# Sparse attention, a 2-D DFT and a two-layer network on one core: values of two query tiles in one task, DFT matmuls of full width, and another order

## The chip, the cores and the metric

The program runs on one core of one Trainium2 chip. The metric is device time in microseconds (us). A time beside a kernel's name is the median of its runs; the profile is of one further execution, whose own time is given with it.

## The reference

Eight batches. Attention first: eight heads of width 64, 32 global and 512 local rows. A global query sees all 544 keys; a local query sees the 32 global keys and the local keys at most 32 rows away.

```python
s_g = scale * np.matmul(q_g, k_all.transpose(0, 1, 3, 2))
out_g = np.matmul(sm(s_g), v_all)
mask = np.abs(pos[:, None] - pos[None, :]) <= window        # window = 32
s_l = np.concatenate([s_lg, np.where(mask, s_ll, -1e9)], axis=-1)
out_l = np.matmul(sm(s_l), np.concatenate([v_g, v_l], axis=2))
```

The 544 x 512 result of a batch then goes through a 2-D Fourier transform of which the real part is kept, a normalisation, and two layers of 2048 and 512 columns:

```python
mixed = np.real(np.fft.fft(np.fft.fft(x, axis=1), axis=2))
u = x + mixed
un = (u - mu) / np.sqrt(var + 1e-06)
out = u + np.maximum(un @ w_ch1, 0.0) @ w_ch2
```

## The kernel before

Every large product is made of three float16 products (high times high, high times low, low times high), so that its accuracy is near float32. The weights come in as 64-bit numbers and are split on the chip.

**Attention.** The unit is a pair of heads (32 pairs, four to a batch). Its 512 local queries are four tiles of 128; two tiles are a half (64 halves). `scores` (L646, L656) multiplies a half's queries with its keys in matmuls that take 64 rows and 64 stationary columns. `masked` (VectorE) and `exps` (ScalarE) follow; for each single tile `p_hi` (ScalarE) and `p_lo` (GpSimd) split the exponentials into `ph`, and `turn` (L688) transposes them by DMA into `pl`. `values` (L691 to L707) multiplies one transposed tile by the values: 20 matmuls with 64 stationary columns each. Two neighbouring `values` write one PSUM bank, `bk`, and `norm` (VectorE) divides a half's result. The next half may write `bk` only after that `norm`. `g_scores` (L734 to L741) and `g_values` (L776) do the same for the global queries of two pairs, with 64 and with 32 stationary columns.

**DFT.** `d_first` (L973, L975) runs five times a batch: four times eight matmuls with 128 stationary columns, and once eight with one column, for the frequency that stands alone. `d_second` (L1003, L1005) runs six times a batch, for three row tiles `kt` and two parts `cs`: row tiles 0 and 1 have 128 stationary columns, row tile 2 has 18. With `cs` 0 it adds one matmul on a constant of 64 rows (`alt`, L1005). `d_as`, `d_df`, `d_addp` and `d_addv` add the result to the input, which makes the rows of the network.

**Network.** These rows come in 17 chunks of 256. VectorE and ScalarE normalise a chunk and split it (`l_hi` is L1075, `l_lo` is L1079), and a DMA transposes it (`l_turn`, L1102). TensorE then runs 16 `f_first` tasks (L1128, 12 matmuls with 256 moving columns) and 16 `f_second` tasks (L1146, 6 matmuls with 512) for each chunk, 272 of each in all, with 128 stationary columns in every matmul.

**What sets the order.** `run` lists all tasks with their engine, an assumed duration, what they need and what they free. `Plan.order` goes through an assumed time line and gives each engine a fixed order; a due time decides between tasks that could start, and the table `BIAS` shifts the due times. Each engine then runs its instructions in exactly that order, and waits where an input is late. The assumed durations thus decide on the order alone.

Of the kernel before, what the change touches and what calls it, by code (L numbers as in the profile page):

```python
# [20 lines left out]
P = 128  # L21
# [33 lines left out]
def shape_constants():  # L55
    r = np.arange(P)[:, None]
    k = np.concatenate([np.arange(1, 144, 2), [0], np.arange(271, 144, -2), np.arange(2, 143, 2), [272, 0], np.arange(270, 143, -2)])[None, :]
    used = np.arange(NK)[None, :] != 72
    tt = np.concatenate([np.arange(129, 144), np.arange(415, 400, -1), [0, 272]])[:, None]
    c1 = np.zeros((P, 2, 2, NK), np.float16)  # L60
    c1t = np.zeros((96, 2, NK), np.float16)
    c2 = np.zeros((P, 2, 2, 2, NH), np.float16)
    for i, fn in enumerate((np.cos, np.sin)):
        for j, a in enumerate(_hi_lo(fn(2 * np.pi * ((r + 1) * k % T) / T) * used)):
            c1[:, i, j] = a
        hi, lo = _hi_lo(fn(2 * np.pi * (tt * k % T) / T) * used)
# [24 lines left out]

def cold(key):

    n, i = key[0], key[1] if len(key) > 1 else 0
    if n == "scores":
        return 2.4 if i < 8 * NRAW else 0.8
    if n == "g_scores":
        return 3.7 if i < 2 * NRAW else 1.2
    if n == "values":
        return 0.8  # L100
    if n == "g_values":
        return 1.1
    return COLD.get(n)
# [16 lines left out]
HALVES = "scores masked exps norm".split()  # L120
QUARTERS = "p_hi p_lo turn p_turn p_copy values".split()
GROUPS = "s_total scales0 scales g_scores g_max g_exp g_hi g_lo g_turn g_copy g_values g_norm".split()


def place(key):

    n, i = key[0], key[1] if len(key) > 1 else 0
    if n in ("load_consts", "l_load"):
        return ("K", 0), 0
    if n in WHOLE:  # L130
# [22 lines left out]
class Plan:  # L153
# [12 lines left out]
    def dues(self):  # L166
        nxt = {k: [] for k in self.tasks}
        for t in self.tasks.values():
            for a in t.data:
                nxt[a].append(t)  # L170
        done = set()
        for root in self.tasks:
            stack = [(root, iter(nxt[root]))]
            if root in done:
                continue
            while stack:
                k, it = stack[-1]
                for n in it:
                    if n.key not in done:
                        stack.append((n.key, iter(nxt[n.key])))  # L180
                        break
                else:
                    stack.pop()
                    if k not in done:
                        done.add(k)
                        t = self.tasks[k]
                        lat = t.dur + (4.0 if t.eng == "SP" else 0.3)
                        t.due = min([t.due] + [n.due - lat for n in nxt[k]])
        for t in self.tasks.values():
            t.due -= t.early + BIAS.get((t.key[0], t.stage), 0) + BIAS.get(t.unit, 0)  # L190

    def order(self):
        self.dues()
        left = {k: len(set(t.after)) for k, t in self.tasks.items()}
        nxt = {k: [] for k in self.tasks}
        for t in self.tasks.values():
            for a in set(t.after):
                nxt[a].append(t)
        engines = ("PE", "DVE", "ACT", "POOL", "SP")
        free = dict.fromkeys(engines, 0.0)  # L200
        ready = {e: [t for t in self.tasks.values() if t.eng == e and not left[t.key]] for e in engines}
        insts, out, dma, bank, t0 = {}, [], 0.0, ("", 0.0), None
        now, count = 0.0, 0
# [47 lines left out]
        while count < len(self.tasks):  # L251
            best = None
            for e in engines:
                low = max(now, free[e])
                if best is not None and low > best[0][0]:
                    continue
                for t in ready[e]:
                    at = max(low, t.base)
                    if best is not None and (at, t.cls, t.due) >= best[0]:
                        continue  # L260
                    at = max(at, ok_at(t))
                    if at < LATE and (best is None or (at, t.cls, t.due) < best[0]):
# [36 lines left out]
class Kern:  # L299
# [64 lines left out]
    def load_consts(self):  # L364
        nc, c = self.nc, self.cp
        for n, shape in (("c1", [P, 2, 2, NK]), ("c1t", [96, 2, NK]), ("c2", [P, 2, 2, 2, NH]), ("alt", [64, NH])):
# [1081 lines left out]
```

## Time and profile before

| | before |
|---|---|
| median of 3 runs | 1026.47 us (1025.48 to 1026.83) |
| profiled execution, its own time | 1026.17 us |
| its span, first to last instruction | 1024.3 us |
| TensorE matmuls busy | 930.3 us (91%) in 12115 matmuls |
| VectorE, ScalarE, GpSimd busy | 528.6, 546.5, 577.9 us |
| granted TensorE clock, mean | 0.953 |

The span is the stretch between the first and the last instruction that were recorded; 1.87 us of the execution's time lie outside it. Matmuls are pipelined, and their recorded durations overlap. What a task takes of TensorE is therefore read here from start to start: the first matmul of the next task minus the first matmul of this one.

### The profile page before, as it was taken

Reading aid. Unit: us, or ns where it says so; the run is one execution under the profiler, and the core shown is the slowest. Engines: PE = TensorE matmul, PEld = TensorE weight load, DVE = VectorE, ACT = ScalarE, POOL = GpSimd, SP = SyncE. Lnnn points to the kernel's source line nnn. Section 1 sums busy time; section 2 is a strip of 40 time slices with the busy share of each in tenths; the row PEclk is TensorE's granted clock in tenths of the full one; section 3 lists DMA queues with packets and bytes.
Section 4 is the critical chain, followed back from the end, with each engine's and each line's share of the span. In section 5 each row is a group of like instructions: output and inputs, shape, how many; then the busy total and the mean of one; then the engine's idle time right before and its main releaser. Section 6 shows DMA issues by size and latency. Waiting matters only on the chain.

```text
span 1024.3 us, 29886 instructions
## 1 busy us (share of the span) xinstructions
PE 930.3 (91%) x12115; PEld 640.3 (63%) x12115; DVE 528.6 (52%) x1609; ACT 546.5 (53%) x1234; POOL 577.9 (56%) x976
## 2 busy tenths in 40 slices
PE   2663459999999999999999999999999999999996
PEld 1442337666666766666676667667667766667673
DVE  5987786147644664446557444783534433221111
ACT  6997768867776656864676667453421311111010
POOL 5599775888868577958757795882416111010000
PEclk9985558999999999999999999999999999999999
DMA  9998998347886566783876797244161201201000
GB/s 334 304 251 235 273 182 187 109 120 134 162 179 151 132 140 151 171 167 105 149 165 130 129 204 162 78 93 103 34 138 48 62 13 53 62 1 42 1 22 21
DMA packets 215794, 133.12 MB, mean 130 GB/s; under 512 B 167808, under 2 KB 185312, under 8 KB 215656
## 3 DMA queue, kind: packets, MB, share of 16 engines
q1 hardware_dynamic: 215656, 131.21, 55.5%
q8 instruction: 95, 1.56, 0.6%
q14 instruction: 43, 0.35, 0.1%
HBM read 64.97 MB, written 18.35 MB: 81 GB/s over the span
## 4 chain that ended last, share of the span: by engine, by line
PE 80%; DMA 6%; DVE 4%; POOL 3%; ACT 2%; SPq 2%; issue 1%; POOLq 0%; ACTq 0%; DVEq 0%
PE ps L1128 34%; PE acc L1146 34%; PE bk L704 3%; DMA vf<-in_v 2%; PE S L656 2%; PE bk L707 1%; PE S L646 1%; DMA raw<-in_moe_w_ch 1%; PE psd L1003 1%; DMA vS<-vN 1%; DMA pl<-ph 1%; PE S L739 1%; PE S L1003 1%; PE psd L973 1%; PE pvg L776 1%
## 5 line engine op out<-in xcount | busy, mean ns | idle before, releaser
L1128 PE MATMUL ps<-uh,wh 128*128 128x256 f16 x3264 | 383.2, 273 | 0.0
L1146 PE MATMUL acc<-wh,h 128*128 128x512 f16 x1632 | 375.1, 379 | 1.5 <-DVE h L1137 1.5
L1128 PEld LDWEIGHTS <-wh 128*128 128x128 f16 x3264 | 313.4, 98 | 52.5 <-issue 1.1
L1146 PEld LDWEIGHTS <-h 128*128 128x128 f16 x1632 | 154.6, 98 | 167.9 <-DVE h L1137 2.0
L1133 ACT ACTIVATE h<-ps 128x512 f16<-128x512 f32 x136 | 81.0, 596 | 289.0 <-PE ps L1128 281.8
L1137 DVE SCALAR_TENSOR_TENSOR h<-ps,h 128x512 f16<-128x512 f32 x136 | 93.7, 689 | 254.5 <-ACT h L1133 254.3
L682 POOL TENSOR_TENSOR ph<-pe,ph 128x256 f16<-128x256 f32 x128 | 86.9, 679 | 46.7 <-ACT ph L678 29.4
L675 ACT ACTIVATE pe<-pe,nm 128x160 f32<-128x160 f32 x256 | 88.0, 416 | 20.2 <-DVE nm L666 20.1
L666 DVE CUSTOM_DVE_ANT_0 pe<-S,msk,z 128x160 f32<-128x160 f32 x192 | 62.2, 379 | 45.3 <-PE S L656 33.6
L704 PEld LDWEIGHTS <-pl 128*64 128x64 f16 x1536 | 47.8, 120 | 39.0 <-issue 23.5
L704 PE MATMUL bk<-vS,pl 128*64 128x65 f16 x768 | 56.7, 208 | 11.7 <-DMA vS<-vN 11.7
L704 PE MATMUL bk<-vN,pl 128*64 128x65 f16 x768 | 56.9, 207 | 8.7 <-DVE x L718 8.1
L596 POOL TENSOR_TENSOR vN<-vf,vN 128x640 f16<-128x640 f32 x32 | 43.7, 1367 | 28.8 <-ACT vN L592 28.7
L678 ACT ACTIVATE ph<-pe 128x320 f16<-128x320 f32 x128 | 55.2, 458 | 8.7 <-DMA pl<-ph 8.6
L1027 POOL TENSOR_TENSOR u<-u,asm 128x257 f32<-128x257 f32 x16 | 13.1, 816 | 75.4 <-DMA u<-xs 44.0
L707 PE MATMUL bk<-vN,pl 128*64 128x65 f16 x1024 | 52.6, 205 | 0.5 <-issue 0.5
L646 PE MATMUL S<-gr,qk 64*64 64x32 f32 x256 | 13.5, 287 | 34.4 <-DVE nm L666 27.4
L683 POOL TENSOR_TENSOR ph<-pe,ph 128x64 f16<-128x64 f32 x128 | 43.6, 341 | 0.0
L707 PEld LDWEIGHTS <-pl 128*64 128x64 f16 x1024 | 42.1, 121 | 0.6 <-issue 0.6
L481 POOL TENSOR_TENSOR wh<-wm,wh 128x512 f16<-128x512 f32 x32 | 36.9, 1159 | 5.5 <-ACT wm L474 3.9
L1151 DVE SCALAR_TENSOR_TENSOR u<-acc,ve,u 128x512 f32<-128x512 f32 x34 | 25.5, 751 | 27.2 <-PE acc L1146 27.0
L620 POOL TENSOR_TENSOR qT<-qk,qT 128x512 f16<-128x512 f32 x24 | 27.9, 1165 | 19.0 <-ACT qT L615 18.9
(212 smaller groups left out, 1492.6 us busy)
## 6 DMA issues: line engine op xcount, KB each, us to landing
qk<-in_qk SPq DMA_DIRECT2D x32, 512.0 KB
vf<-in_v SPq DMA_DIRECT2D x32, 320.0 KB
raw<-in_moe_w_ch SPq DMA_DIRECT2D x17, 512.0 KB
vS<-vN SPq DMA_DIRECT2D x64, 130.0 KB
xs<-x SPq DMA_DIRECT2D x32, 256.0 KB
out<-u SPq DMA_DIRECT2D x16, 512.0 KB
x<-xs SPq DMA_DIRECT2D x24, 256.0 KB
u<-xs SPq DMA_DIRECT2D x24, 256.0 KB
```

The source lines that it names most:

```text
L596: self.nc.gpsimd.tensor_sub(vN[:, :, 1, :, 0:64], self.st[p]["vf"], vN[:, :, 0, :, 0:64])
L666: nc.vector.tensor_tensor_reduce(self.per[(4 * p + j) % 4][:, h], S[:, h, 160 * n:160 * n + 160], self.msk[:, j], z[:, 8:9], 3e38, op0=ALU ...
L675: nc.scalar.activation(pe[:, h], pe[:, h], AF.Exp, bias=nm[:, n, h:h + 1], scale=-1.0)
L678: self.nc.scalar.activation(self.phr[i % NPH][:, :, 96:256], self.per[i % 4], AF.Copy)
L682: self.nc.gpsimd.tensor_sub(ph[:, :, 256:384], pe[:, :, 32:160], ph[:, :, 128:256])
L683: self.nc.gpsimd.tensor_sub(ph[:, :, 64:96], pe[:, :, 0:32], ph[:, :, 96:128])
L704: nc.tensor.matmul(pv[r, j % 2, h], pl[:, 3 * h + 1 + a, r], v, start=x == 0, stop=False)
L707: nc.tensor.matmul(pv[r, j % 2, h], pl[:, 3 * h, r], vN[:, 4, c, h], start=False, stop=c == 1)
L1128: nc.tensor.matmul(ps[:, q], wt[:, w, c0:c0 + P], uh[:, :, 4 * a + kt, :], start=n == 0, stop=n == 11)
L1133: self.nc.scalar.activation(h[:, 0], self.fps[c, fp], AF.Relu)
L1137: self.nc.vector.scalar_tensor_tensor(h[:, 1], self.fps.pop((c, fp)), 0.0, h[:, 0], op0=ALU.max, op1=ALU.subtract)
L1146: nc.tensor.matmul(self.acc_f[c, j], h[:, a, q, j * P:(j + 1) * P], self.w[1, f][:, w, :], start=f == 0 and a == 0 and w == 0, stop=f == 1 ...
```

## The change

Two neighbouring `values` become one task of 40 matmuls, which needs both transposed tiles. The transposed tiles get six buffers instead of four.

```diff
-        self.st[p]["pl", j] = pl = self.p3.tile([P, 6, P], F16, name="pl", bufs=4)
+        self.st[p]["pl", j] = pl = self.p3.tile([P, 6, P], F16, name="pl", bufs=6)
     def values(self, i):
-        nc, (p, j) = self.nc, divmod(i, 4)
+        nc, (p, half) = self.nc, divmod(i, 2)
...
+        for n in range(2):
+            j = 2 * half + n
+            pl = s.pop(("pl", j))
...
-                    nc.tensor.matmul(pv[r, j % 2, h], pl[:, 3 * h, r], vN[:, 4, c, h], start=False, stop=c == 1)
+                        nc.tensor.matmul(pv[r, n, h], pl[:, 3 * h, r], vN[:, 4, c, h], start=False, stop=c == 1)
```

In the DFT the lone frequency and row tile 2 are computed with 128 stationary columns, of which the same one and 18 result rows are used as before; the constants `alt` and `zr` get 96 rows, the added ones zero.

```diff
-    alt = np.zeros((64, NH), np.float16)
+    alt = np.zeros((96, NH), np.float16)
-        self.zr = c.tile([64, NK], F16, name="zr")
+        self.zr = c.tile([96, NK], F16, name="zr")
-                nc.tensor.matmul(po, eh[:, a, e:e + m], self.c1[:, cs, c, c0:c0 + n], start=k == 0, stop=False)
+                nc.tensor.matmul(po, eh[:, a, e:e + P], self.c1[:, cs, c, c0:c0 + n], start=k == 0, stop=False)
-                nc.tensor.matmul(po, z[:, a, o, k0:k0 + r], self.c2[:, cs, o, c, :], start=n == 0, stop=n == 2 and cs + o > 0)
+                nc.tensor.matmul(po, z[:, a, o, k0:k0 + P], self.c2[:, cs, o, c, :], start=n == 0, stop=n == 2 and cs + o > 0)
-                nc.tensor.matmul(po, self.zr[:, k0:k0 + r], self.alt, start=False, stop=True)
+                nc.tensor.matmul(po, self.zr[:, k0:k0 + P], self.alt, start=False, stop=True)
```

The order counts a change between the groups `scores`, `values`, `g_scores`, `g_values` and everything else as extra TensorE time, some assumed durations differ, the biases of chunk tasks share one entry, and the weights' transfers get units of their own. The table of biases is a new one throughout.

```diff
+FORM = {"scores": 1, "values": 2, "g_scores": 3, "g_values": 4}
+TURN = 0.105
+            if e == "PE" and FORM.get(t.key[0], 0) != form:
+                form = FORM.get(t.key[0], 0)
+                t.dur += TURN if t0 is not None else 2 * TURN
-BIAS = {('load_consts', 0): -57, ('K', 0): -100, ('w_load', 0): 112, ...
+BIAS = {('load_consts', 0): 246, ('K', 0): -151, ('w_load', 0): 102, ...
```

Line numbers of the kernel after are higher by 9 in the attention's preparation, by 8 at `g_values`, and by 11 at `d_second` and the network.

TensorE, row tile 2 of the DFT of batch 2 with `cs` 0 (`z0` is its stationary operand, `zr` the constant's, `wh` the network's weights), before:

```order
L1003 LDWEIGHTS z0_6009
L1003 MATMUL S_6414<-c2r_172,z0_6009 18x129
...
L1005 LDWEIGHTS zr_176
L1005 MATMUL S_6414<-altr_174,zr_176 18x129
...
L1128 LDWEIGHTS wh_1050
L1128 MATMUL ps1_6426<-uh_4468,wh_1050 128x256
```

After:

```order
L1014 LDWEIGHTS z0_6162
L1014 MATMUL psd_6561<-c2r_164,z0_6162 128x129
...
L1016 LDWEIGHTS zr_168
L1016 MATMUL psd_6561<-altr_166,zr_168 128x129
...
L473 MATMUL bk_131<-vac1_78,part_64 128x6
L1139 LDWEIGHTS wh_1155
L1139 MATMUL ps1_6450<-uh_4339,wh_1155 128x256
```

The first number of a matmul's shape is its stationary columns. The 18 have become 128, in the DFT's matmuls and in that on the constant.

TensorE, two `values` of one half at the start of chunk 2 (`pl` are the transposed tiles), before:

```order
L704 LDWEIGHTS pl_4225
L704 MATMUL bk_131<-vN_70,pl_4225 64x65
...
L1128 LDWEIGHTS wh_741
L1128 MATMUL ps1_4387<-uh_4059,wh_741 128x256
...
L704 LDWEIGHTS pl_4236
L704 MATMUL bk_131<-vN_70,pl_4236 64x65
```

After, a half that stands between two tasks of the network:

```order
L712 LDWEIGHTS pl_4871
L712 MATMUL bk_131<-vN_70,pl_4871 64x65
...
L712 LDWEIGHTS pl_4973
L712 MATMUL bk_131<-vS_71,pl_4973 64x65
...
L1139 LDWEIGHTS wh_1155
L1139 MATMUL ps1_5300<-uh_4037,wh_1155 128x256
```

Before, one `f_first` stood between the two tiles; after, the second tile's matmuls follow the first's without anything between.

ScalarE, the last instructions up to the second half of chunk 0 (L1075; `kT`, `kg`, `qk` and `qT` are the keys and queries of batch 2), before:

```order
L605 ACTIVATE qk2_97<-qk2_97,z_1971 128x512
L397 ACTIVATE ps1_2226<-raw_2138 128x512
L1075 ACTIVATE unh_2230<-un_2219 128x512
L402 ACTIVATE raw_2138<-raw_2138 128x512
L615 ACTIVATE qT_2235<-qk2_97 128x512
L626 ACTIVATE kg1_69<-gT_946,z_1971 128x64
L605 ACTIVATE qk0_95<-qk0_95,z_1971 128x512
L1075 ACTIVATE unh_2322<-un_2300 128x512
```

After (L1086 is that instruction now):

```order
L1021 ACTIVATE asm_2141<-psd_2076,dsc_1451 18x258
L1086 ACTIVATE unh_2144<-un_2138 128x512
L687 ACTIVATE ph_84<-pe1_86 128x2x160
L547 ACTIVATE junk_76,vac0_77<-vf1_73 128x640
L547 ACTIVATE junk_76,vac0_77<-qk0_95 128x512
L406 ACTIVATE ps1_2170<-raw_2013 128x512
L1086 ACTIVATE unh_2180<-un_2167 128x512
```

The preparation of batch 2's queries and keys stands behind chunk 0's second half now, no longer ahead of it.

## Rows read from the trace of the kernel before

**Rows 1.** Windows: busy time by engine, clock, DMA share and GB/s.

```profile
0.00:50.00 50.00, 22.73 (x430) 16.56 (x430) 36.02 (x118) 39.23 (x88) 27.83 (x56) 1.00 1.05 318
100.00:150.00 50.00, 24.12 (x404) 18.14 (x397) 41.44 (x100) 37.38 (x83) 38.40 (x57) 0.50 1.03 241
157.00:1015.00 858.00, 854.53 (x10690) 583.10 (x10688) 405.84 (x1233) 425.00 (x961) 460.63 (x797) 1.00 0.49 107
1015.00:1024.30 9.30, 0.00 (x0) 0.00 (x0) 0.37 (x1) 0.00 (x0) 0.00 (x0) 0.74 0.18 56
```

**Rows 2.** Waits of TensorE from 157 to 1015: total, times, longest.

```profile
PE acc L1146 <- DVE h L1137: 1.5, 1, 1.5
```

**Rows 3.** Timeline, network at the end: start, us, what, count.

```profile
1003.99 5.40 PE L1128 MATMUL ps<-uh,wh 128*128 128x256 f16 x48
1009.23 5.34 PE L1146 MATMUL acc<-wh,h 128*128 128x512 f16 x24
```

**Rows 4.** Timeline, TensorE at the start of chunk 2.

```profile
257.74 1.48 PE L1128 MATMUL ps<-uh,wh 128*128 128x256 f16 x12
259.15 0.22 PE L704 MATMUL bk<-vN,pl 128*64 128x65 f16 x1
...
259.59 0.61 PE L1128 MATMUL ps<-uh,wh 128*128 128x256 f16 x4
```

**Rows 5.** Timeline, TensorE, batch 2's DFT and a `g_scores` ahead of it.

```profile
338.63 0.41 PE L739 MATMUL S<-kT,gT 128*64 128x512 f16 x2
...
339.48 0.34 PE L1003 MATMUL psd<-c2r,z 128*128 128x129 f16 x3
339.76 0.23 PE L1005 MATMUL psd<-altr,zr 64*128 64x129 f16 x1
339.92 0.34 PE L1003 MATMUL psd<-c2r,z 128*128 128x129 f16 x3
...
343.55 0.51 PE L1003 MATMUL psd<-c2r,z 128*128 128x129 f16 x6
343.90 1.47 PE L1128 MATMUL ps<-uh,wh 128*128 128x256 f16 x12
...
347.99 0.51 PE L1003 MATMUL psd<-c2r,z 128*128 128x129 f16 x6
348.43 0.34 PE L1003 MATMUL S<-c2r,z 128*18 128x129 f16 x3
...
349.13 1.48 PE L1128 MATMUL ps<-uh,wh 128*128 128x256 f16 x12
```

**Rows 6.** Timeline, TensorE, two `values` in one visit; a `g_values`.

```profile
288.94 0.22 PE L704 MATMUL bk<-vN,pl 128*64 128x65 f16 x1
...
289.70 0.27 PE L646 MATMUL S<-kg,qT 64*64 64x32 f16 x12
...
297.07 0.66 PE L776 MATMUL pvg<-vN,plg 128*32 128x65 f16 x60
297.65 0.22 PE L704 MATMUL bk<-vN,pl 128*64 128x65 f16 x1
```

**Rows 7.** TensorE's weight loads by line and shape: busy, mean ns, idle before.

```profile
L1003 PEld LDWEIGHTS <-z 128*128 128x128 f16 x192 | 13.6, 103 | 5.8 <-issue 2.1
L1003 PEld LDWEIGHTS <-z 128*18 128x18 f16 x96 | 5.5, 94 | 4.5 <-issue 3.6
```

**Rows 8.** ScalarE by line and shape from 0 to 157.

```profile
L605 ACT ACTIVATE qk<-qk,z 128x512 f32<-128x512 f32 x4 | 2.8, 712 | 0.0
L615 ACT ACTIVATE kT<-qk 128x512 f16<-128x512 f32 x2 | 1.2, 625 | 0.0
L626 ACT ACTIVATE kg<-gT,z 128x64 f16<-128x64 f16 x2 | 0.7, 331 | 0.0
```

**Rows 9.** Timeline: transposes of chunks 0 and 2 on SP's queue, first network matmuls.

```profile
150.88 1.23 SPq L1102 DMA_TRANSPOSE uh<-unh  x1
156.47 2.74 PE L1128 MATMUL ps<-uh,wh 128*128 128x256 f16 x12
242.82 4.14 SPq L1102 DMA_TRANSPOSE uh<-unh  x2
```

**Rows 10.** Waits from 0 to 157: total, times, longest.

```profile
PE bk L704 <- DMA vS<-vN: 11.7, 1, 11.7
```

More of the change, by code (lines that the diff above doesn't have):

```diff
@@ L95, in cold @@
     if n == "scores":
-        return 2.4 if i < 8 * NRAW else 0.8
+        return 2.1 if i < 8 * NRAW else 0.9
     if n == "g_scores":
@@ L99, in cold @@
     if n == "values":
-        return 0.8
+        return 1.3
     if n == "g_values":
@@ L119 @@
 PAIRS = "load load_v load_vb sums_q sums_k sums_v mul_k hi_k lo_k mul_q hi_q lo_q halo v_mul v_hi v_lo v_out x_square x_out".split()
-HALVES = "scores masked exps norm".split()
-QUARTERS = "p_hi p_lo turn p_turn p_copy values".split()
+HALVES = "scores masked exps values norm".split()
+QUARTERS = "p_hi p_lo turn".split()
 GROUPS = "s_total scales0 scales g_scores g_max g_exp g_hi g_lo g_turn g_copy g_values g_norm".split()
@@ L129, in place @@
         return ("K", 0), 0
+    if n == "w_load":
+        return ("W", i // 4), i // 2
     if n in WHOLE:
@@ L189, in dues @@
         for t in self.tasks.values():
-            t.due -= t.early + BIAS.get((t.key[0], t.stage), 0) + BIAS.get(t.unit, 0)
+            t.due -= t.early + BIAS.get(("f", 0) if t.key[0][0] == "f" else (t.key[0], t.stage), 0) + BIAS.get(t.unit, 0)
     def order(self):
@@ L202, in order @@
         insts, out, dma, bank, t0 = {}, [], 0.0, ("", 0.0), None
-        now, count = 0.0, 0
+        now, count, form = 0.0, 0, 0
         LATE = 1e18
@@ L972, in d_first @@
                 e = base + kp * w + d0
-                nc.tensor.matmul(po, eh[:, a, e:e + m], self.c1[:, cs, c, c0:c0 + n], start=k == 0, stop=False)
+                nc.tensor.matmul(po, eh[:, a, e:e + P], self.c1[:, cs, c, c0:c0 + n], start=k == 0, stop=False)
             e = (0, 129, 257, 385)[2 * cs + o] + d0
-            nc.tensor.matmul(po, ht[:, e:e + m], self.c1t[:, cs, c0:c0 + n], start=False, stop=True)
+            nc.tensor.matmul(po, ht[:, e:e + P], self.c1t[:, cs, c0:c0 + n], start=False, stop=True)
     def d_z(self, b, i):
@@ L1264, in run @@
                 else:
-                    add(("scores", i), PE, .5, self.scores, i, after=[("lo_q", p), ("lo_k", p), ("halo", p)], seq=sq, use=[qT, kT, kg], new=[S], **kw)
+                    add(("scores", i), PE, .43, self.scores, i, after=[("lo_q", p), ("lo_k", p), ("halo", p)], seq=sq, use=[qT, kT, kg], new=[S], **kw)
                 add(("masked", i), DVE, 1.3, self.masked, i, after=[("scores", i)], use=[S] if rb else [S, sc], new=[nm] + pers, **kw)
@@ L1273, in run @@
                     add(("turn", u), SP, 1.3, self.turn, u, after=[("p_lo", u)], seq=pu("turn"), use=[ph], new=[pl], kb=380, **kw)
-                    add(("values", u), PE, .37, self.values, u, after=[("turn", u), ("v_out", p)], seq=pu("values") + ([("norm", i - 1)] if u % 2 == 0 and i else []), use=[pl, vN, bk], **kw)
                 x = ("x", p)
-                add(("norm", i), DVE, .89, self.norm, i, after=[("values", 2 * i), ("values", 2 * i + 1)], use=[bk, sc] + ([x] if half else []), new=[] if half else [x], **kw)
+                add(("values", i), PE, .64, self.values, i, after=[("turn", 2 * i), ("turn", 2 * i + 1), ("v_out", p)], seq=[("norm", i - 1)] if i else [], use=[("pl", 2 * i), ("pl", 2 * i + 1), vN, bk], **kw)
+                add(("norm", i), DVE, .89, self.norm, i, after=[("values", i)], use=[bk, sc] + ([x] if half else []), new=[] if half else [x], **kw)
             if p % 2:
@@ L1283, in run @@
                     gs, gu = [(n, i) for n in ("lo_k", "halo") for i in two] + [("b_lo", b)], [(n, i) for n in ("kT", "kg") for i in two] + [gT]
-                add(("g_scores", g), PE, 1.9 if rb else .8, self.g_scores, g, after=gs, seq=pg("g_scores"), use=gu, new=[G], alts=[["A"], ["acc0", "acc1"]], **kw)
+                add(("g_scores", g), PE, 1.9 if rb else .7, self.g_scores, g, after=gs, seq=pg("g_scores"), use=gu, new=[G], alts=[["A"], ["acc0", "acc1"]], **kw)
                 add(("g_max", g), DVE, 1.08, self.g_max, g, after=[("g_scores", g)], use=[G] if rb else [G, sc], **kw)
@@ L1290, in run @@
                 pvg, xg = ("tr", "g", g), ("xg", b)
-                add(("g_values", g), PE, .95, self.g_values, g, after=[("g_turn", g)] + [("v_lo", i) for i in two], seq=pg("g_values"), use=[("plg", g)] + [("vN", i) for i in two], new=[pvg], **kw)
+                add(("g_values", g), PE, .8, self.g_values, g, after=[("g_turn", g)] + [("v_lo", i) for i in two], seq=pg("g_values"), use=[("plg", g)] + [("vN", i) for i in two], new=[pvg], **kw)
                 add(("g_norm", g), DVE, .7, self.g_norm, g, after=[("g_values", g)], seq=pg("g_norm") if g % 2 else [], use=[pvg, sc] + ([xg] if g % 2 else []), new=[] if g % 2 else [xg], **kw)
@@ L1331, in run @@
                 pre = [base, ("d_tail_lo", b)] + ([("d_first", b, i - 1)] if i else [("load_consts",)])
-                add(("d_first", b, i), PE, .65, self.d_first, b, i, after=pre, use=[eh, ht], new=[ps], alts=banks, **kd)
+                add(("d_first", b, i), PE, .52, self.d_first, b, i, after=pre, use=[eh, ht], new=[ps], alts=banks, **kd)
                 add(("d_z", b, i), ACT, .48, self.d_z, b, i, after=[("d_first", b, i)], use=[ps] + ([] if new else [z]), new=new, **kd)
@@ L1340, in run @@
                     pre = [before] + [("d_z2", b, 2 * cs + o) for o in range(2)] + ([("d_z2", b, 4)] if cs == 0 else [])
-                    add(("d_second", b, kt, cs), PE, .55, self.d_second, b, kt, cs, after=pre, use=[(f"z{cs}", b)] + ([("zr", b)] if cs == 0 else []), new=[ps], alts=banks, **kd)
+                    add(("d_second", b, kt, cs), PE, .40, self.d_second, b, kt, cs, after=pre, use=[(f"z{cs}", b)] + ([("zr", b)] if cs == 0 else []), new=[ps], alts=banks, **kd)
                     before = ("d_second", b, kt, cs)
@@ L1382, in run @@
                 for q in range(2):
-                    add(("f_first", c, fp, q), PE, 1.3, self.f_first, c, fp, q, after=([("f_first", c, fp, 0)] if q else [("l_lo" if c < NLT else "l_turn", c, j) for j in range(2)] + col + prv),
+                    add(("f_first", c, fp, q), PE, 1.31, self.f_first, c, fp, q, after=([("f_first", c, fp, 0)] if q else [("l_lo" if c < NLT else "l_turn", c, j) for j in range(2)] + col + prv),
                         use=[uh] + ([ps] if q else []), new=[] if q else [ps], cls=8, due=T)
```

37 lines of the change are left out of this document (18 added, 19 removed).

## The prediction

> **What bounds the kernel now.** I read the windows first, then TensorE's waits, then its timeline, and last the weight loads and the stretch before the network. The windows cut the span in three. From 157 to 1015 TensorE is busy 854.53 of 858 us at the full granted clock (2.4 GHz), while VectorE, ScalarE and GpSimd are busy about half of it [rows 1]. TensorE's waits agree: the longest of that stretch is 1.5 us [rows 2]. Up to 157 no engine is full, DMA engines are at 0.95 to 1.05, VectorE and ScalarE are busy 36 to 42 of each 50 us and TensorE about half, from 100 on at 0.50 of the clock, the 1.2 GHz level [rows 1]. After 1015 come 9.30 us in which the last result is added and stored [rows 1]. So three sums set the time: when the network starts (156.47 [rows 9]), how much TensorE has to do from there, and a tail that the change doesn't touch. Work taken from TensorE after 156.47 comes off the end, as long as the next chunk is there in time.
>
> A busy TensorE isn't one that multiplies all the time, so I read it from start to start. In the plain network 48 matmuls of L1128 take 1009.23 - 1003.99 = 5.24 us, 12 of them 1.31 [rows 3].
>
> **The price of a change of form.** By form I mean the tile of the array that a matmul names: 128 stationary columns, 64, 32, 18 or 1, and 64 or 128 rows. The same 12 matmuls of L1128 ahead of a `values` take 259.15 - 257.74 = 1.41 us [rows 4], 0.10 more than in the network alone. One tile of `values` and the way out take 259.59 - 259.15 = 0.44 us [rows 4], two tiles in one visit 289.70 - 288.94 = 0.76 [rows 6]; a tile alone is thus 0.32 and the way out 0.12. In the DFT six matmuls with 128 columns take 343.90 - 343.55 = 0.35 us when L1128 follows, 58 ns each, and there is no extra although line, operands and PSUM tile all change [rows 5]. Where 18 columns follow, the same six take 348.43 - 347.99 = 0.44, 0.09 more. Three of them ahead of the 64-row constant take 0.28 instead of 0.17, and that one matmul 0.16 instead of 0.06 [rows 5]. So a change costs 0.09 to 0.12 us, and only a change of form does. I take 0.095: it is nearest to the rows of L1128 and L1003, which stand at most of the changes.
>
> **How many go.** I counted changes between rows of TensorE's order, from the first L1128 to the end: 333 before, 219 after. Of the 114 that go, 79 lie inside the DFT of the seven batches after that point (the lone frequency, row tile 2, and the constant, in and out), where none is left. The other 35 are visits: 254 changes between the attention's matmuls and the rest become 219, since a half's two tiles are visited once. 114 x 0.095 = 10.8 us; by the ends of the price 10.3 to 13.7. As a check on one task: row tile 2 with the constant takes 349.13 - 348.43 = 0.70 us and costs 0.09 more ahead of it [rows 5]; seven matmuls at 58 ns are 0.41, so 0.38 goes, four changes at 0.095. All this lies on the path, since TensorE waits for nothing there.
>
> **Wider stationary operands.** 21 matmuls a batch (8 of the lone frequency, 13 of row tile 2) load 128 columns instead of 1 or 18. Loads of 128 columns are recorded with 103 ns, of 18 with 94 [rows 7], and they lie beside matmuls: with 128 columns these still start every 58 ns [rows 5]. I take nothing; if the whole 9 ns showed it would be 21 x 7 x 0.009 = 1.3 us. The Trainium skill says otherwise (TensorE: Matmul & The Clock Gate, "LDWEIGHTS (loading the stationary operand)"): a load takes its columns divided by 1.2 GHz, estimated 107 ns for 128 and 15 for 18. By that rule wider operands would cost time where the matmuls between are short; the trace disagrees, with 103 against 94 ns, and by the trace's 58 ns the sum stays as it is.
>
> **What crosses the network's start.** Ahead of the first L1128 stand 480 matmuls of `values` instead of 520, and one `g_scores` and one `g_values` fewer. They come behind it: two tiles at 0.32; a `g_scores`, 339.48 - 338.63 = 0.85 less its way out of 0.10 [rows 5]; a `g_values`, 297.65 - 297.07 = 0.58 less 0.10 [rows 6]. Together +1.9 us.
>
> **When the network starts.** The new table moves nearly everything before it. Ahead of chunk 0's second L1075 ScalarE no longer has batch 2's preparation: four scalings at 0.712, three splits at 0.625, two copies at 0.331 [rows 8], together 5.4 us. SP's queue has as many rows ahead of chunk 0's second transpose, 133, but with one more pair of heads to load (832 KB) and one copy of values (260 KB) fewer; 0.83 MB at the 241 to 318 GB/s of that stretch [rows 1] are 2.6 to 3.4 us if all of it delays. ScalarE isn't full there, so its 5.4 us don't all come off. Bounds: 5.4 earlier to 3.4 later. I take 1.5 earlier, a little past the middle, because VectorE and GpSimd have no more work ahead of that point either.
>
> **Added waits.** A `values` of 40 matmuls needs both tiles, and the in-order queue behind it (the `scores` of the next half, the network) stands while the second is missing. After 157 the chunk work hides this little: TensorE had only 3.5 us of idle in all [rows 1]. The six buffers let a tile land two tasks ahead. No gain here is possible beyond the 3.5; for the cost the nearest row is the 1.5 us wait [rows 2], once in each of a few batches. I take +1.0, between -3 and +8.
>
> **The sum.** 1026.17 (the profiled execution) - 10.8 + 1.9 - 1.5 + 1.0 = 1016.8. The median is 0.3 above the profiled execution, so 1017 us, 0.9% faster.
>
> **Rivals.** *A chunk that comes late.* Chunk 2's two transposes are issued from 242.82 on within 4.14 us; chunk 0's took at most 156.47 - 150.88 = 5.6 us from issue to the first matmul [rows 9]. That leaves 257.74 - 246.96 - 5.6 = 5.2 us of slack, and a faster TensorE arrives earlier, while the DFT that feeds the chunk also passes VectorE, GpSimd and SP. For it: the new order may have used up the slack at the even chunks, which follow their DFT closest. Against it: the DFT's own matmuls get shorter. With 2 to 4 us lost at two of them the time is 1021 to 1025, say 1022.5.
>
> *A start held up, slower than before.* Before 157 TensorE's queue already stood 11.7 us at one `values`, for the copy of the values [rows 10]. Twelve halves now stand there, each waiting for both tiles, with `scores` behind them, and VectorE and ScalarE live on `scores`. One more stop of that size, on top of the copy's, moves the start by 11.7 instead of -1.5: 1017 + 13.2 = 1030. It decides from 9 us of delay on, and is slower than the old time by over 0.2% from about 13. Against it: SP's rows ahead of chunk 0 are no more, and the merged task is no later than its later half was.
>
> *The DFT keeps its cost.* If the extra 0.09 belonged to the small result and not to its form, only the 35 visits would count: 7.5 us less of a gain, 1024.5. Against it stands the 128-column task with the 64-row constant, which pays too [rows 5]; for it, that no row shows the lone frequency with 128 columns.
>
> *Loads that bind.* If a matmul behind each wide load started only every 103 ns [rows 7] instead of 58, 147 matmuls would lose 45 ns each, 6.6 us: 1023.6. The 58 ns at 128 columns [rows 5] speak against it. This is the way of the Trainium skill's rule on LDWEIGHTS named above.
>
> **How the numbers follow.** The forecast holds 0.65, with its own range 1010 to 1022; the late chunk 0.17; the held-up start 0.10; the DFT's cost kept 0.05; binding loads 0.03. The low end, 1009, has the start 5.4 earlier and a change at 0.11. The high end, 1025, has the start 3.4 later or the late chunk at its worst; beyond it lie most of the held-up start and little else. About 0.2% (2 us) is what a measurement of this kernel can tell from no change. Faster by more: 0.63 of the forecast, 0.15 of the late chunk, 0.05 of the rest, together 0.83. Slower by more: most of the held-up start, 0.09. In between 0.08.
>
> **What would show it.** Right: six or seven DFT matmuls of L1014 at 58 ns wherever they stand, no extra at L1016; the L1139 ahead of a merged `values` still at 1.41; the stretch from the first network matmul to the last shorter by 7 to 11 us. The start is right between 151 and 160. Wrong on the waits: idle rows of TensorE at L712 or at a chunk's first L1139 that sum to more than 5 us. The forecast fails if the start is past 165, or if the DFT's changes of form cost nothing to begin with.

## The result and the profile after

The changed kernel takes 1011.76 us (median of 4 runs, 1010.80 to 1013.39), the kernel before 1026.65 (4 runs, 1025.48 to 1027.01). The ratio is 0.9859, 95% interval 0.9841 to 0.9876: 1.4% faster, 14.9 us, where 9.5 were forecast. The direction and the range (1009 to 1025) held; half of the gain came at the start of the network, to which the sum had given 1.5 us.

Both profiled executions can be cut at the first and the last network matmul's start:

| us | before | after | difference | forecast |
|---|---|---|---|---|
| start of the network | 156.47 | 149.13 | -7.34 | -1.5 |
| first to last network matmul | 857.73 | 850.58 | -7.15 | -7.9 |
| from there to the end of the span | 10.11 | 9.76 | -0.35 | 0 |

(The forecast for the stretch is -10.8 + 1.9 + 1.0.)

Windows of the kernel after, with the columns of [rows 1]:

```profile
130.00:145.00 15.00, 7.69 (x132) 6.06 (x132) 14.65 (x48) 12.32 (x33) 9.20 (x17) 0.65 1.14 269
149.00:1000.00 851.00, 845.36 (x10810) 586.76 (x10806) 408.56 (x1242) 430.26 (x969) 470.22 (x808) 1.00 0.49 108
```

The main stretch is still TensorE's, busy 845.36 of 851 us at the full granted clock. TensorE waits more than before, 5.7 us instead of 1.5 [rows 2]; its waits from 149 to 1000 (total, times, longest):

```profile
PE bk L712 <- DVE x L726: 3.7, 3, 1.7
PE bk L473 <- ACT junk L547: 1.0, 1, 1.0
PE pvg L784 <- DVE wsc L461: 1.0, 1, 1.0
```

Three of them stand at a `values` of 40 matmuls (L712) whose result bank was still being read out. No L1139 waits for a turned chunk. TensorE's timeline in batch 2's DFT answers to [rows 5]:

```profile
345.04 0.51 PE L1014 MATMUL S<-c2r,z 128*128 128x129 f16 x6
...
347.53 0.34 PE L1014 MATMUL psd<-c2r,z 128*128 128x129 f16 x3
347.71 0.22 PE L1016 MATMUL psd<-altr,zr 96*128 96x129 f16 x1
347.77 0.34 PE L1014 MATMUL psd<-c2r,z 128*128 128x129 f16 x3
```

Three matmuls ahead of the constant take 347.71 - 347.53 = 0.18 us, before 0.28; the constant 0.06, before 0.16. A wide matmul takes 58 ns; what made the narrow ones dear were the changes around them. A two-tile `values` behind the network, TensorE's timeline:

```profile
161.86 2.79 PE L1139 MATMUL ps<-uh,wh 128*128 128x256 f16 x24
164.58 0.22 PE L712 MATMUL bk<-vN,pl 128*64 128x65 f16 x1
...
270.91 0.22 PE L712 MATMUL bk<-vN,pl 128*64 128x65 f16 x1
...
271.66 2.76 PE L1157 MATMUL acc<-wh,h 128*128 128x512 f16 x12
```

24 L1139 take 164.58 - 161.86 = 2.72 us; at [rows 3]'s 0.109 each they would take 2.62, so the 0.10 at a `values` is as it was [rows 4]. The two tiles take 0.75 with the way out, as two in one visit did before, 0.76 [rows 6]. The price of a change has not moved; there are fewer of them.

Now the start. SyncE's timeline, chunk 0's two transposes (before: [rows 9]), and TensorE's first network matmul:

```profile
143.68 2.69 SPq L1113 DMA_TRANSPOSE uh<-unh  x2
```

```profile
149.13 2.61 PE L1139 MATMUL ps<-uh,wh 128*128 128x256 f16 x12
```

They are issued by 146.37; before, the second was issued from 150.88. One place where chunk 0 was held is GpSimd. Its timeline before, and VectorE's step ahead of it (L1020 ends the DFT's first row tile, L1027 adds it to the chunk):

```profile
133.43 0.48 DVE L1020 SCALAR_TENSOR_TENSOR asm<-psd,dsc,asm 128x258 f32<-128x258 f32 x1
```

```profile
135.79 0.80 POOL L584 TENSOR_SCALAR vf<-vf,z 128x640 f32<-128x640 f32 x1
136.56 1.15 POOL L620 TENSOR_TENSOR kT<-qk,kT 128x512 f16<-128x512 f32 x1
...
138.56 0.73 POOL L1027 TENSOR_TENSOR u<-u,asm 128x257 f32<-128x257 f32 x1
```

The input is there at 133.91; the sum runs at 138.56, behind batch 2's scaling of values and splitting of keys (L584, L620) and rounded probabilities. After:

```profile
132.83 0.47 DVE L1031 SCALAR_TENSOR_TENSOR asm<-psd,dsc,asm 128x258 f32<-128x258 f32 x1
```

```profile
133.38 0.73 POOL L1038 TENSOR_TENSOR u<-u,asm 128x257 f32<-128x257 f32 x1 [0.32 <-DVE asm L1031]
```

The sum waits 0.32 us for its input and follows at once. From 130 to 145 GpSimd is busy 9.20 us (the first window above), where before it was busy 13.44:

```profile
130.00:145.00 15.00, 7.32 (x117) 5.35 (x116) 13.20 (x37) 13.56 (x30) 13.44 (x24) 0.50 1.18 238
```

The order after has ten of GpSimd's steps, twelve of ScalarE's, one `g_values` of TensorE's and five of VectorE's fewer ahead of chunk 0's second rounding. Among VectorE's is the joining of the last weight tile.

Chunk 0 alone did not set the start, though. Ahead of the first network matmul stands the last weights' fold in TensorE's queue: a matmul that brings the largest weights of all rows, which VectorE has picked out, onto one row. Behind it come two tiles of `values`. TensorE's timeline at the fold and a window of all engines (columns as above), before:

```profile
154.92 0.37 PE L438 MATMUL vm<-ident,mx 128*1 128x128 f32 x1 [1.57 <-DVE xg L786]
```

```profile
153.50:154.80 1.30, 0.00 (x0) 0.00 (x0) 1.20 (x6) 0.64 (x2) 0.00 (x0) 0.50 0.00 0
```

After, with the first matmul of `values`:

```profile
146.93 0.37 PE L447 MATMUL vm<-ident,mx 128*1 128x128 f32 x1 [0.16 <-DVE mx L441]
147.88 0.21 PE L712 MATMUL bk<-vN,pl 128*64 128x65 f16 x1 [0.58 <-DVE x L726]
```

```profile
147.90:148.60 0.70, 0.70 (x27) 0.70 (x28) 0.70 (x3) 0.67 (x2) 0.70 (x2) 0.50 0.00 0
```

Before, no DMA engine moved anything from 153.5 to 154.8, so chunk 0's transposes had landed by 153.5; TensorE stood idle until VectorE had divided the result of a `g_values` (L786), and the network began 3.0 us after chunk 0 lay ready. After, the transposes had landed by 147.9, and the network again began behind fold and `values`. So two chains meet at the first network matmul, and both came earlier: the landing by 5.6 us, the fold by 8.0. VectorE's last step of joining the last weight tile (L414, now L423) and its part of chunk 0's second rounding (L1079, now L1090), before and after:

```profile
149.12 0.69 DVE L414 SCALAR_TENSOR_TENSOR wm<-raw,ps 128x512 int32<-128x512 int32 x1
149.73 1.12 DVE L1079 TENSOR_TENSOR unh<-un,unh 128x512 f16<-128x512 f32 x1
```

```profile
143.59 0.68 DVE L1090 TENSOR_TENSOR unh<-un,unh 128x512 f16<-128x512 f32 x1
...
145.51 0.69 DVE L423 SCALAR_TENSOR_TENSOR wm<-raw,ps 128x512 int32<-128x512 int32 x1
```

Before, 5.1 us of VectorE's queue lay between the end of that joining (149.81) and the fold, with chunk 0's second rounding and the `g_values` result in it; after, 0.7.

### The profile page after: what moved, and what is told of

It reads as the page before. It is cut to its first block, busy times and chain, and to the rows that moved or that the text cites. A ratio compares the mean times of both kernels' runs of the same rounds, so it can differ in the third digit from the quotient of the medians.

```text
span 1009.5 us, 29862 instructions
## 1 busy us (share of the span) xinstructions
PE 912.9 (90%) x12115; PEld 638.9 (63%) x12115; DVE 526.5 (52%) x1609; ACT 548.0 (54%) x1234; POOL 579.7 (57%) x976
## 4 chain that ended last, share of the span: by engine, by line
PE 76%; DMA 8%; DVE 5%; ACT 3%; issue 2%; POOL 2%; SPq 2%; POOLq 0%; ACTq 0%; DVEq 0%
PE ps L1139 33%; PE acc L1157 32%; PE bk L712 2%; PE S L665 2%; DMA raw<-in_moe_w_ch 2%; DMA x<-xs 1%; DMA pl<-ph 1%; DMA vf<-in_v 1%; PE S L655 1%; PE bk L715 1%; DMA qk<-in_qk 1%; DMA xs<-x 1%; PE psd L1014 1%; ACT pe L684 1%; DVE ps L422 1%
## 5 line engine op out<-in xcount | busy, mean ns | idle before, releaser
L1139 PE MATMUL ps<-uh,wh 128*128 128x256 f16 x3264 | 383.3, 273 | 0.0
L1139 PEld LDWEIGHTS <-wh 128*128 128x128 f16 x3264 | 315.9, 98 | 56.4 <-issue 0.4
L712 PE MATMUL bk<-vN,pl 128*64 128x65 f16 x768 | 53.9, 206 | 16.7 <-DVE x L726 9.4
L712 PEld LDWEIGHTS <-pl 128*64 128x64 f16 x1536 | 47.1, 119 | 29.8 <-issue 17.3
L712 PE MATMUL bk<-vS,pl 128*64 128x65 f16 x768 | 53.6, 206 | 1.4 <-DMA pl<-ph 1.4
L715 PE MATMUL bk<-vN,pl 128*64 128x65 f16 x1024 | 50.5, 204 | 0.0
L726 DVE TENSOR_TENSOR x<-bk,dn 128x256 f32<-128x256 f32 x64 | 27.2, 424 | 22.1 <-DMA xs<-x 18.4
L1118 POOL TENSOR_TENSOR ve<-ve 128x2 f32<-128x2 f32 x17 | 7.7, 450 | 49.2 <-DVE ve L1076 49.1
```

The source lines that it names most:

```text
L712: nc.tensor.matmul(pv[r, n, h], pl[:, 3 * h + 1 + a, r], v, start=x == 0, stop=False)
L715: nc.tensor.matmul(pv[r, n, h], pl[:, 3 * h, r], vN[:, 4, c, h], start=False, stop=c == 1)
L1139: nc.tensor.matmul(ps[:, q], wt[:, w, c0:c0 + P], uh[:, :, 4 * a + kt, :], start=n == 0, stop=n == 11)
```

## The experiments

The kernels before and after differ in three things: the wide DFT, the two-tile task with its buffers, and the order. Theory at the outset: each change of form costs what the prediction says, in the DFT as between visits, and the start moved because ScalarE was relieved. Rivals: a change inside the DFT is free and visits alone count; another step sets the start. "Stretch" is from the first to the last network matmul's start.

**The wide DFT alone, old order.**

```diff
-    alt = np.zeros((64, NH), np.float16)
+    alt = np.zeros((96, NH), np.float16)
...
-            nc.tensor.matmul(po, ht[:, e:e + m], self.c1t[:, cs, c0:c0 + n], start=False, stop=True)
+            nc.tensor.matmul(po, ht[:, e:e + P], self.c1t[:, cs, c0:c0 + n], start=False, stop=True)
...
```

> The kernel before with the DFT's matmuls at 128 stationary columns and constants of 96 rows, in the old order and with single values. Theory (only a change of form costs, about 0.095 us): 79 changes go, the stretch from the first to the last network matmul falls from 857.7 by 7 to 8 us to about 850, the start stays at 156.5 within 1 us, and the time is about 1019. Rival (the extra belongs to the small result): the stretch stays at 857 and the time at 1026. Rival (wide loads bind): 147 matmuls lose 45 ns each against the theory, stretch about 857, with L1014 matmuls 100 ns apart.

Measured: 1018.25 us, ratio 0.9922 (0.9908 to 0.9937). Stretch 849.97, 7.76 shorter; start 156.35, unmoved. Its row tile 2, from TensorE's timeline:

```profile
342.73 0.51 PE L1006 MATMUL psd<-c2r,z 128*128 128x129 f16 x6
343.08 1.47 PE L1131 MATMUL ps<-uh,wh 128*128 128x256 f16 x12
```

All intervals from start to start between two DFT matmuls, and between a DFT and a network matmul, summed behind the network's start: 48.79 us before, 41.20 here. That is 7.59 us for 79 changes, 0.096 each. The rival that the DFT keeps its cost is refuted, and with it the loads that bind.

**The two-tile visits alone, old order, six buffers.**

```diff
+        held = None
         for t in self.order():
-            t.fn(*t.args, *([t.alt] if len(t.alts) > 1 else []))
+            if t.key[0] == "values" and t.key[1] % 2 == 0:
+                held = t
+                continue
+            for t in ([held, t] if t.key[0] == "values" else [t]):
+                t.fn(*t.args, *([t.alt] if len(t.alts) > 1 else []))
...
```

> The kernel before with six transposed buffers and each first tile's values moved directly ahead of the second tile's; all else in the old order. It has 27 changes between attention matmuls and the rest fewer after the start (254 to 227). Theory: the stretch falls by 27 x 0.095 = 2.6 us to about 855; the start stays within 1.5 us. Rival (the merged task holds up the queue at the start): the start moves later by 3 us or more. Rival (visits do not matter): the stretch stays within 1 us of 857.7.

Measured: 1024.23 us, ratio 0.9983 (0.9971 to 0.9994). Stretch 856.94, only 0.79 shorter with 27 changes fewer; start 155.59. TensorE's waits tell why:

```profile
PE acc L1151 <- DVE h L1142: 1.7, 1, 1.7
PE psd L1008 <- ACT asm L1015: 1.5, 1, 1.5
PE bk L712 <- issue: 1.0, 1, 1.0
```

Of every interval that lies more than 0.25 us above the median of its kind, what lies above counts here as a wait. So counted, waits grew by 1.4 to 2.8 us, by how finely kinds are told apart; without them the stretch is 2.2 to 3.6 us shorter, 0.08 to 0.13 for each of the 27. Merging saves its changes and hands most back as waits when the order isn't made for it.

**ScalarE's preparation of batch 2 put behind chunk 0**, which is the reason that the prediction gave for an earlier start. What hangs on it goes along: three of GpSimd's splits and a `g_scores`.

```diff
-        for t in self.order():
+        for t in behind(self.order(), [(n, q) for n in ("mul_k", "hi_k", "mul_q", "hi_q", "halo") for q in (8, 9)], ("l_hi", 0, 1)):
...
```

> The kernel before with the preparation of batch 2's queries and keys (twelve ScalarE and GpSimd tasks, and one global score) moved behind chunk 0's second split; all else in the old order. Theory A (ScalarE's 5.4 us of preparation held up chunk 0): the start moves from 156.5 to 151 to 153. Rival B (ScalarE waited for weights, and VectorE's later chain sets the start): the start stays within 1.5 us of 156.5.

Measured: 1026.03 us, ratio 1.0001 (0.9991 to 1.0011), start 155.81. The second rounding of chunk 0 ended at 149.21 instead of 150.85, 1.6 us earlier; the fold came at 154.26 and the start only 0.7 earlier. The reason falls.

**A weight tile's steps put behind the DFT's first way out.**

```diff
-        for t in self.order():
+        for t in behind(self.order(), [("w_abs", 28), ("w_low", 28)], ("d_as", 0, 0)):
...
```

> The kernel before with the four steps of weight tile 28 (two on ScalarE that wait for its transfer until 130.4, two on VectorE) moved behind the DFT's first asm of batch 0; all else in the old order. Theory B (the DFT of batch 0 stood behind a weight transfer in ScalarE's queue): the first asm moves from 132.5 to about 129.5 and the start comes 2 to 3 us earlier. Rival A (preparation held it up): the asm moves and the start stays within 1 us of 156.5.

Measured: 1026.71 us, ratio 1.0006 (0.9995 to 1.0017). The DFT's way out came 2.0 us earlier (130.5), the start 1.0 (155.49) instead of 2 to 3, and the time did not change. As the reason for the 7.3 us it is refuted. Kernels whose order is the same up to the start (the kernel after and the two grouped ones below) differ there by 0.6 us.

**The kernel after with the narrow DFT.** The edit of the first experiment, undone in the changed kernel:

```diff
-            nc.tensor.matmul(po, ht[:, e:e + P], self.c1t[:, cs, c0:c0 + n], start=False, stop=True)
+            nc.tensor.matmul(po, ht[:, e:e + m], self.c1t[:, cs, c0:c0 + n], start=False, stop=True)
...
```

> The changed kernel, its order as it is, with the DFT's matmuls back at 18 or 1 stationary columns and 64 rows. Theory (a change of form costs 0.095 to 0.11 us beside the network, and the DFT alone held 79 of them): the stretch from the first to the last network matmul comes back by 7.5 to 8.5 us, from 850.6 to 858 to 859; the start stays within 1 us of 149.1, because the wide DFT has no part in it; time about 1019.5 us, 0.7 to 0.8% above the changed kernel. Rival (the wide DFT is what let chunk 0 come earlier): the start goes back to 153 or later, time 1023 or more.

Measured: 1021.75 us, ratio 0.9946 (0.9930 to 0.9963). Start 147.53. So an early start doesn't need the wide DFT (here it is narrow), and neither the wide DFT nor the two-tile visits bring it on the old order (above, both late): of the change's parts the new order is left. Whether it could do so without the two-tile visits for which it was made was not run. The DFT's intervals grew by 7.5 us, as expected; the stretch by 12.6, which was not. TensorE's timeline shows the rest:

```profile
497.85 2.78 PE L1136 MATMUL ps<-uh,wh 128*128 128x256 f16 x24
...
502.89 0.19 PE L712 MATMUL bk<-vN,pl 128*64 128x65 f16 x1 [2.27 <-DVE x L726]
505.45 0.59 PE L473 MATMUL bk<-vac,part 128*128 128x6 f32 x2 [1.73 <-ACT junk L547]
505.90 5.28 PE L1136 MATMUL ps<-uh,wh 128*128 128x256 f16 x24
```

Two waits stand close together, and the 24 matmuls behind them take 5.28 us instead of 2.78. The windows (columns as above) say why:

```profile
500.00:505.00 5.00, 1.45 (x46) 1.13 (x44) 0.42 (x1) 1.88 (x5) 4.66 (x4) 1.00 0.96 347
505.00:511.50 6.50, 6.05 (x28) 4.28 (x29) 1.56 (x6) 3.97 (x11) 4.31 (x12) 0.50 0.41 129
512.00:516.00 4.00, 4.00 (x26) 2.43 (x25) 1.29 (x2) 4.00 (x7) 2.52 (x3) 1.00 0.30 67
```

TensorE was busy 1.45 of 5 us, and the granted clock then fell to 0.50, the 1.2 GHz level, until 511.8. Against the same intervals at the full clock that is 3.1 us. The remaining 2.0 are longer waits (1.7 to 2.3 by the count above).

**Two changes of form put back into each merged visit.** An extra matmul of 65 columns, its result unused, stands between the two tiles: with 128 stationary columns it changes form twice, with 64 it does not.

```diff
+            if n:
+                nc.tensor.matmul(self.bk[0:128, 300:365], pl[:, 0, 0:128], vN[:, 4, 0, 0], start=True, stop=True)
...
+                nc.tensor.matmul(self.bk[0:64, 300:365], pl[:, 0, 0:64], vN[:, 4, 0, 0], start=True, stop=True)
```

> The changed kernel with one more matmul of 65 columns and 128 stationary columns between the two tiles of each merged visit of values, its result left unused: two changes of form more in each of 52 visits, and 52 matmuls more. Theory (price by the change of form, 0.095 to 0.12 us): the stretch grows by 10 to 12 us more than in the same kernel with 64 columns in the extra matmul, time about 1024 us. Rival (the saved time came from fewer visits, their waits and buffers, and a change of form is free): both grow alike, by 1.5 to 3 us, time about 1014 us.

> The control: the same extra matmul of 65 columns with 64 stationary columns, the form of its neighbours, so no change of form is added. Theory and rival alike: 52 matmuls at 0.03 to 0.06 us, 1.5 to 3 us, time about 1014 us; only if an extra matmul costs by itself more than 0.1 us does the difference to the one with 128 columns say less.

Measured: 1021.41 us, ratio 0.9951 (0.9933 to 0.9969), with 128 columns; 1014.12, ratio 0.9864 (0.9817 to 0.9911), with 64. One visit of each on TensorE's timeline, first with 128 (L709 is the extra matmul):

```profile
258.94 0.22 PE L714 MATMUL bk<-vN,pl 128*64 128x65 f16 x1
...
259.38 0.20 PE L709 MATMUL bk<-vN,pl 128*128 128x65 f16 x1
259.51 0.22 PE L714 MATMUL bk<-vS,pl 128*64 128x65 f16 x1
...
259.95 2.76 PE L1159 MATMUL acc<-wh,h 128*128 128x512 f16 x12
```

and with 64:

```profile
256.09 0.22 PE L714 MATMUL bk<-vN,pl 128*64 128x65 f16 x1
...
256.43 0.20 PE L709 MATMUL bk<-vN,pl 128*64 128x65 f16 x1
...
256.88 0.82 PE L1159 MATMUL acc<-wh,h 128*128 128x512 f16 x3
```

The visit takes 1.01 against 0.79 us, 0.11 for each change; over all merged visits the intervals between `values` matmuls sum to 45.90 against 34.10 us, 11.8 for 104 changes. The medians differ by 7.3 only, and in the profiled executions the stretch by no more than 3.2 (859.79 against 856.63), where 10 to 12 were expected: the slower TensorE waits less, 1.8 us against 8.4 by the lists of waits. The theory holds in the price and missed in the sum: a change of form taken away is paid in full only where nothing then comes late. (The runs with 64 columns lie between 1010.08 and 1016.85, and the profiled one is the longest.)

**Chunk 0's own steps emitted as early as their inputs allow, in the kernel before.**

```diff
-        for t in self.order():
+        for t in ahead(self.order()):
...
+CHAIN = [("d_df", 0, 0), ("d_addp", 0, 0), ("d_addv", 0, 0), ("l_guess", 0)] + [(n, 0, j) for n in ("l_stats", "l_un", "l_hi", "l_lo") for j in (0, 1)]
...
```

> The kernel before, with chunk 0's own steps (the DFT's differences and sums, the statistics, the scaling and the two roundings of both halves) emitted as early as their inputs allow, ahead of later chunks' preparation and weight steps in the queues of VectorE, GpSimd and ScalarE; nothing else moved. Theory C (the in-order queues held chunk 0 back, GpSimd's sum at 138.56 though its input was there at 133.9): the sum runs near 134 and the start of the network comes 3 to 6 us earlier than 156.5, time 1021 to 1024 us. Rival D (the last weights and their fold in TensorE's queue set the start): chunk 0's roundings come earlier, the start stays within 1 us of 155.5 to 156.5, time 1026 us.

Measured: 1029.43 us, ratio 1.0025 (1.0007 to 1.0044), start 160.2. GpSimd's sum ran at 134.9 and the second rounding ended at 142.39 instead of 150.85, as theory C said, and the network began later all the same. SyncE's timeline and waits (130 to 162):

```profile
154.85 3.42 SPq L1121 DMA_TRANSPOSE uh<-unh  x2
```

```profile
SPq L707 <- PE bk L726: 7.9, 2, 6.5
```

ScalarE now stood for chunk 0's rounding with the DFT's second way out queued behind it; TensorE waited for that, SyncE's queue for TensorE, and chunk 0's transpose stood in SyncE's queue. So did the last weight tile's load, issued at 147.0 instead of 138.4, and the fold came at 158.4.

**Moved only past what it stood behind**, twice: the second version mends what the first showed standing still.

```diff
+MOVES = [
+    ([('d_addp', 0, 0)], ('mul_k', 8)),
+    ([('l_stats', 0, 0), ('l_stats', 0, 1), ('l_guess', 0)], ('w_bits', 29)),
+    ([('l_un', 0, 0), ('l_hi', 0, 0), ('l_lo', 0, 0), ('l_un', 0, 1)], ('w_abs', 30)),
...
+    ([('f_first', 0, 0, 0)], ('scores', 15)),
+]
```

and in the second, in the place of the lines with `w_bits` and `w_abs`:

```diff
+    ([('w_bits', 29), ('w_join', 29), ('l_stats', 0, 0), ('l_stats', 0, 1), ('l_guess', 0), ('l_un', 0, 0)], ('d_df', 0, 1)),
+    ([('w_abs', 30), ('w_low', 30), ('l_hi', 0, 0), ('norm', 10), ('l_lo', 0, 0), ('l_un', 0, 1), ('w_bits', 30), ('w_join', 30), ('l_hi', 0, 1), ('l_lo', 0, 1), ('d_df', 0, 1)], ('values', 22)),
```

> The kernel before, its DFT and values as they were, with the steps of chunk 0 each moved in its own queue only past what it was seen to stand behind: GpSimd's sum past five steps of batch 1 and 2, VectorE's statistics past a weight tile's joining, ScalarE's roundings past the last weight tiles, which wait for their loads, SyncE's two turns past the way out of values, and the first network matmul past a scores task and the last weights' fold. Theory (the order of chunk 0's chain in all five in-order queues sets the start, and is what the change's new order gave): the second rounding ends near 142.5 instead of 150.85, the turn lands near 148, start 147.5 to 151, stretch as before within 1.5 us, time 1018 to 1022 us. Rival (the last weights' arrival and joining set it): start 154 or later, time 1025 us or more.

> The kernel before once more with chunk 0's steps moved, mended where the run e9_untied showed them stand still: weight tile 30, whose buffer the turned tile takes over, is joined in the gaps of chunk 0's rounding and not behind it, one tile's way out goes ahead of the first rounding, no weight tile that is still being loaded stands ahead of a rounding on ScalarE, and the last weights' fold stands directly ahead of the first network matmul. DFT and values as before. Theory (the order in the five in-order queues alone can give the start): second rounding ends near 145, turn lands near 149, start 148.5 to 151.5, stretch 857 to 861, time 1017 to 1022 us. Rival (something besides the order, such as the merged visits or the wide DFT, is needed): start 154 or later.

Measured: 1030.79 us, ratio 1.0032 (1.0018 to 1.0046), start 155.40; and 1028.02, ratio 1.0004 (0.9988 to 1.0020), start 154.84. Both missed, in the stretch too: 864.18 and 860.22. In the first the transposes were issued from 150.94, when weight tile 30 had given up their buffer, and TensorE, with the fold now behind the first network matmul, stood 4.5 us for chunk 0. In the second both were issued by 149.36, the old ones by 150.88 + 1.23 = 152.11 [rows 9], and the network's first matmul stood in TensorE's queue behind a `g_values` and the fold (154.68). SyncE, then TensorE's waits from 130 to 158:

```profile
146.75 2.61 SPq L1120 DMA_TRANSPOSE uh<-unh  x2
```

```profile
PE pvg L794 <- POOL vN L614: 5.7, 1, 5.7
```

Its values were rounded late because GpSimd stood 6.2 us for a step of the DFT that I had put back. Before, the last `g_values` ahead of the network ran at 146.5; in the kernel after it is at 99.9.

**More of the same saving**, tried on the kernel after: attention tasks held back past at most three (four) network tasks, to stand next to each other.

```diff
-        for t in self.order():
+        for t in later(self.order()):
...
+LATER = [
+    (('values', 13), ('values', 14)),
+    (('scores', 16), ('g_scores', 4)),
...
```

> The changed kernel with 25 attention tasks, and the steps that hang on each, held back past at most three network tasks, so that they stand directly ahead of the next attention task: 35 changes of form fewer behind the start, 219 to 184. By the price of a change (0.095 to 0.12 us) 3.3 to 4.2 us less, some of it lost to waits of steps that now come late: time 1008 to 1010.5 us. Rival (the waits for late steps eat all): 1011 us or more.

> As the run before, but held back past at most four network tasks, 32 attention tasks moved: 45 changes of form fewer, 219 to 174, by the price 4.3 to 5.4 us less; its later steps wait more: time 1007 to 1010.5 us. Rival (the waits for late steps eat all): 1011 us or more.

Measured: 1030.29 us, ratio 1.0031 (1.0018 to 1.0044), and 1034.22, ratio 1.0066 (1.0051 to 1.0081): 18 and 22 us slower than the kernel after, with 35 and 45 changes fewer. TensorE's waits of the first, from 149 to 1010:

```profile
PE S L698 <- DVE nm L718: 12.4, 9, 1.6
PE bk L755 <- DVE x L769: 5.6, 6, 1.2
PE S L790 <- DVE nm L718: 2.8, 2, 1.4
```

Where two `scores` stand side by side, the second waits about 1.4 us for VectorE to read the one bank they share; a change of form saves 0.1. The network work between them was the cover. The kernel after stayed the fastest of all that ran.

## Why the prediction was right, and where not

- **The price of a change: right.** 0.095 was taken, between 0.09 and 0.12. The runs show 0.096 in the DFT (79 changes, 7.59 us) and 0.11 at `values` (104 changes, 11.8 us). By these the 114 changes are 7.6 + 35 x 0.11 = 11.4 us, forecast 10.8.
- **Wider operands cost nothing: right.** The L1014 matmuls start every 58 ns wherever they stand, while their loads of 128 columns are recorded with 98 ns (the median in the kernel after). The Trainium skill (TensorE: Matmul & The Clock Gate, "LDWEIGHTS (loading the stationary operand)") states that a load takes its columns divided by 1.2 GHz. That is, as an estimate, 107 ns for 128 columns; the trace comes near that, but such a load holds up no matmul here.
- **Work that crosses the start: taken over, not measured by itself.** With it the stretch adds up: -11.4 + 1.9 + 2.2 (waits) = -7.3; measured -7.15. By the count of e3_pairs the waits grew by 2.1 to 2.8 us, so the 1.9 is known to no better than half a us.
- **Added waits: right in direction and, for the most part, in place, too small.** 3.7 of the 5.7 us stand at L712, as said, but for the result bank's way out, not for a tile that is missing. They cost 2.1 to 2.8 instead of 1.0, inside the bounds.
- **When the network starts: the term that was mis-sized.** Forecast 1.5 earlier, bounds 5.4 earlier to 3.4 later, "right between 151 and 160"; it came 7.3 earlier, at 149.13, past the bound. Two things failed in that step. The prediction put the time into ScalarE's 5.4 us of preparation, and that alone moved the start by 0.7 and the time by nothing (1.0001). And it said that VectorE and GpSimd had "no more work ahead of that point either", and stopped there: both had less. On GpSimd chunk 0's sum stood 4.7 us with its input ready; on VectorE the last weight tile's joining went ahead of chunk 0's second rounding, and the fold, on which the first network matmul hung as well, came 8.0 us earlier. A bound from one engine's work isn't a bound where five in-order queues feed the start.
- **The rivals.** No chunk came late: no L1139 in the list of waits. The held-up start did not occur. The kept cost and the binding loads are refuted by the wide DFT alone.
- **The range: held, in part by luck.** Its low end doesn't follow from what was named for it: a start 5.4 earlier and a change at 0.11 give 1017 - 3.9 - 1.7 = 1011.4, not 1009. The measured 1011.76 stays within the range although the start came past its bound, and larger waits than forecast took some of that back. In the held-up start, 0.2% over the old time is reached from 10 us of delay (1018.5 + 10), not 13.

Shown: neither the wide DFT nor the two-tile visits move the start by themselves, and with the new order it is early. Open: which moves of it are enough. Five edits of the old order, four of them at the very steps the trace named, moved it by -1.6 to +3.7 us. The traces show why one chain is not enough. In the kernel before and in four runs on its order (e1_wide, e3_pairs, e4_prep, e5_weights) the network begins 1.5 to 1.6 us behind the fold, while chunk 0's second rounding ends anywhere from 149.2 to 150.9. When chunk 0's steps were moved, something else was late: SyncE's queue and the fold (e8_chain), a buffer (e9_untied), a `g_values` and the fold behind it (e12_untied2). What the new order has that none of these edits had is batch 2's preparation, the last `g_values` ahead of the network with the result that VectorE divides, and the last weight tile's joining all behind chunk 0's second rounding at once; that this suffices was argued, not run.

## What to carry to other kernels

Where one engine is full, count its changes of tile form between matmuls and price them from start to start: at 0.1 us each, padding a narrow operand to the neighbours' form was worth 7.6 us here and showed no cost. Bringing visits together pays only as far as the work between them isn't the cover of a shared bank. For a prologue on in-order queues, go back from the first matmul that has to start, list every chain that meets there and what stands ahead of its steps on each engine, and look for the one that ends last. A step that runs late with its input ready is only a candidate: here chunk 0's second rounding came 8.5 us earlier (e8_chain), and the start 3.7 later.

## What the runs showed of the hardware

The granted clock can be lost in the middle of a full stretch. With the narrow DFT TensorE was busy 1.45 of 5 us; the clock then fell to 0.50 for some 6.8 us and cost 3.1. In the kernel after, the waits at the same two places were 1.3 and 1.0 us, and it stayed at 1.00:

```profile
494.00:500.00 6.00, 3.83 (x66) 3.17 (x64) 1.65 (x4) 3.41 (x10) 5.76 (x5) 1.00 0.99 321
```

And a float32 sum over partitions (L473, recorded as two matmuls) takes 0.14 us to the next start when it stands behind network matmuls, 0.24 behind `values`, where the form changes, and 0.19 behind a DFT matmul of the same form (at 347.95 in the kernel after). The first difference is the price of a change; why the DFT makes one of 0.05 is open.
